# Windowed attention and a gated MLP on one core: accumulator banks as single tiles, and the first entry's loads in another order

## The chip, the cores and the metric

The kernel runs on one core of one Trainium2 chip. The metric is the device time of one execution in microseconds (us); lower is better. Engines: PE is TensorE (PEld its weight loads), DVE VectorE, ACT ScalarE, POOL GpSimd; SP is SyncE, whose queue here issues every transfer.

## The reference

```python
batch, n_heads, seq, head_dim = 8, 8, 576, 64
n_tokens, d_model, d_ff = 4608, 512, 2048
scores = q @ k.T / sqrt(64)
rel = pos[:, None] - pos[None, :]
plain   = (rel >= 0) & (rel < 32)                        # heads 0 to 3
dilated = (rel >= 0) & (rel < 128) & (rel % 4 == 0)      # heads 4 to 7
attn = softmax(where(mask, scores, -1e9))
x = (attn @ v), heads side by side: 4608 x 512
h = x @ w_in
out = (h * sigmoid(1.702 * h)) @ w_out
```

All inputs are float32.

## The kernel before

**Attention.** Heads are taken in pairs, one in each half of the partitions: 4 pairs for each of 8 batch entries. The host has reordered the dilated heads, so that both masks are bands. A score block is 32 queries by the 64 keys that its band can reach; `scores(k)` makes 18 such blocks per head and adds the mask by a matmul with the identity (`ident`). `softmax(k)` then takes the maxima (`mx`), subtracts them (`pr`), and takes exponentials, sums (`sm`) and quotients; two transposes (`ct`) and eight copies lay the result out as `bt`, which `product(k)` multiplies by values in windows of 96 keys for 64 queries (`av`, with a rest in the bank `sp`). `drain_x` writes x: for the first entry it is split at once into a high part `xh` and a low part `xl`.

**MLP.** Weights and activations are used as sums of a high and a low part in a faster matmul format, three matmuls for one product. Weights come as raw 64-bit words into buffers (`cell`, `second`), and `decode(n)` splits them with ACT and DVE: even n are blocks of w_in (`wih`, `wil`), odd n of w_out (`woh`, `wol`). The tokens make nine groups: eight of 512 (`m0` to `m7`, one per entry) and one of the eight rests of 64 (`r`). For each of 16 blocks f, `up(f)` makes 12 matmuls into the bank `hp`; `tanh`, `gate`, `hi_g` and `lo_g` make `gh` and `gl`; `down(f)` then adds 8 matmuls with `gh` and 4 with `gl` (the low parts) to the four results of the group, `acc`, which stand in four banks. PE does `up(f+1)` ahead of `down(f)`. At the last block each result is finished and drained (`ost`) in turn, and stored.

**Order.** All of it is written as operations with costs, keys that they read and write, and an urgency; `Plan.ordered` plays them through once at build time and emits each engine's instructions in the order that comes out. The waits between engines are then put in by the framework, by tile. In the first 30 us of the plan, idle stretches of PE are filled with matmuls on the identity (`warm`, written to the tile `idle`). Transfers all stand in SP's queue, in the plan's order. The first group's matmuls run while entry 1's attention and the rest of the weights are worked on.

**Places that the change touches.** The four results are halves of two tiles of two banks; in the first entry the scores of a pair use one of these tiles for both heads. Queries and keys of the first entry alternate between a buffer of their own (`qk`) and the unused space of `second` and `xm`; the values of pairs 1 to 3 lie in `second`, `xm` and `xr` until these are needed.

Of the kernel before, what the change touches and what calls it, by code (L numbers as in the profile page):

```python
# [17 lines left out]
P = 128  # L18
NC = DM // P
NF = DF // P  # L20
GT = 512
# [14 lines left out]
class Plan:  # L36
# [29 lines left out]
    def ordered(self, warm, warm_until):  # L66
# [21 lines left out]
        while any(open_):  # L88
            when, e = min((min(start(i, e) for i in open_[e]), e) for e in range(5) if open_[e])
            here = [i for i in open_[e] if start(i, e) <= when]  # L90
            i = min(here, key=lambda i: ops[i][1])
            e = min((k for k in ops[i][0] if start(i, k) <= when), key=lambda k: abs(ops[i][0][k]))
            for k in ops[i][0]:
                open_[k].remove(i)
            cost = abs(ops[i][0][e])
            if e == PE and when < warm_until:
                idle = max(0, int((when - max(free[e], 1.2)) / (0.24 if when > 5.0 else 0.44)))
                order.extend([(None, e)] * idle)
            order.append((i, e))
            if e == POOL or (e == DVE and ops[i][0][e] < 0):  # L100
                port[0] = when + cost

            free[e] = when + (cost if e != DMA else 0.7 if cost < 100 else 0.43)
            if e == DMA:
                bus[0] = max(bus[0], when + 2.0) + cost / 360.0
                cost = bus[0] - when
            for j in users[i]:
                for to in ready[j]:
                    gap = 0.0 if to == e == PE else 0.13 if to == e else LATENCY[to]
                    ready[j][to] = max(ready[j][to], when + cost + gap + ops[j][4])  # L110
                wait[j] -= 1
                if not wait[j]:
                    for to in ops[j][0]:
                        open_[to].add(j)
# [4 lines left out]
def tile_windowed_attention_then_gated_mlp(  # L119
# [92 lines left out]
    def decode(n, urgency):  # L212
# [42 lines left out]

    nq, nv = S, 2 * NW * D
    spare = [second.bitcast(F32).rearrange("p j n -> p (j n)"), xm.rearrange("p c n -> p (c n)"),
             xr[:, 1:].rearrange("p b c n -> p (b c n)")]
    late_v = words.bitcast(F32).rearrange("p j n -> p (j n)")
# [3 lines left out]
    def lots(k):  # L263

        if k < NC:
            return f"qk{k % 2}", f"v{k}"
        return ("qk0", "v0") if k < FIRST * NC or k % 2 == 0 else ("qk1", "v1")

    def load_qk(k):
        u, place = pairs[k], lots(k)[0]  # L270

        def work(e):
            if place == "qk0":
                flat = temp([P, 2 * nq], F32, "qk", f"qk_{k}")
                both = [flat[:, 0:nq], flat[:, nq:]]
            else:
                both = [spare[a][:, nv:nv + nq] for a in range(2)] if k < NC else [spare[0][:, nq * a:nq * a + nq] for a in range(2)]
            u["q"], u["k"] = both
            if k and place == "qk0":
                load(flat.rearrange("p (a s) -> p a s", a=2), qk[k])  # L280
                return
            for rows in (slice(0, D), slice(D, P)) if k == 0 else (slice(0, P),):
                for a in range(2):
                    load(both[a][rows], qk[k, rows, a])

        add({DMA: 590}, k, work, waits(k), (place,))

    def load_v(k):
        u, place = pairs[k], lots(k)[1]

        def work(e):
            if place == "v0":
                flat = temp([P, nv], F32, "v", f"v_{k}")
            else:
                flat = spare[k - 1][:, 0:nv] if k < NC else late_v[:, 0:nv]
            u["v"] = flat.rearrange("p (a m d) -> p a m d", a=2, m=NW)
            load(u["v"][0:KW], vp[k])

        add({DMA: 442}, k, work, waits(k), (place,))

# [16 lines left out]
    def scores(k):  # L317
        u = pairs[k]
        u["sp"] = sp = bank([P, 2, GT], f"acc{k % 2}" if k < NC else "sp", f"sp_{k}")
        u["boxes"] = sp[:, :, 0:QT * W].rearrange("p a (t w) -> p a t w", t=QT)  # L320
        for a in range(2):
            if masked(k):
                T.matmul(u["boxes"][:, a], ident, mask if dilated(k) else plain, start=True, stop=False,
                         skip_group_check=True)
        for t in range(QT):
            for a, j in [(a, j) for a in range(2) for j in range(min(4, S // 32 - 4 * t))]:
                g, rows = 4 * t + j, slice(D * a, D * a + D)
                dst, keys = u["boxes"][32 * j:32 * j + 32, a, t], u["k"][rows]
                for w in (0, 32) if g == 0 else (0,):
# [5 lines left out]
    def softmax(k, urgency):  # L335
# [6 lines left out]
        def sp():  # L342
            return u["boxes"] if masked(k) else pr

# [3 lines left out]
        if not masked(k):  # L348
            mine = mask if dilated(k) else plain
            for n, tiles, cost in ((P, slice(0, QT - 1), 0.62), (D, slice(QT - 1, QT), 0.22)):  # L350
                add({DVE: cost}, urgency, lambda e, n=n, tiles=tiles: pair(
                    e, pr[0:n, :, tiles], u["boxes"][0:n, :, tiles],
                    mine[0:n, None, tiles].broadcast_to([n, 2, tiles.stop - tiles.start, W]), ALU.add),
                    score_banks(k), (PR,))
        add({DVE: 0.80}, urgency, lambda e: V.tensor_reduce(out=mx, in_=sp(), axis=AX.X, op=ALU.max),
            (*held, PR), (MX,))
        add({DVE: 0.80}, urgency, lambda e: pair(e, pr, sp(), across(mx), ALU.subtract), (*held, MX), (PR,))
        add({ACT: 0.75}, urgency, lambda e: A.activation(pr, pr, AF.Exp, scale=0.125), (), (PR,))  # L358
# [30 lines left out]
    def product(k):  # L389
# [7 lines left out]
        for m in range(NW):  # L397
            for a in range(2):
                rows = slice(D * a, D * a + D)
                dst = u["av"][rows, D * m:D * m + D] if m < NW - 1 else u["rest"][rows]  # L400
                T.matmul(dst, u["v"][0:KW, a, m], bt[0:KW, a, m], start=True, stop=True, skip_group_check=True)  # L401

# [5 lines left out]
    def drain_x(k, urgency):  # L408

        u, (b, c) = pairs[k], divmod(k, NC)  # L410
        freed = ("v2", "qk1") if b == 1 else ()

# [28 lines left out]
        for n, (part, src, other) in enumerate(rests):  # L441
            add({ACT: 0.22}, urgency, lambda e, part=part, src=src: copy(
                e, part(view(xr[:, b, c])), src()), (banks[other],), (f"xr{b}{c}.{n}", *(("v3",) if b == 1 else ())))

# [35 lines left out]
    class Group:  # L480
# [180 lines left out]
```

## Time and profile before

| | before |
|---|---|
| median of 3 runs | 930.05 us (929.17 to 931.56) |
| profiled execution | 926.54 us, of which the span is 924.8 |
| PE busy | 893.0 us, 97% of the span |
| PE weight loads | 721.5 us |
| DVE busy | 520.9 us |
| ACT busy | 322.1 us |
| moved by DMA | 61.97 MB, 67 GB/s over the span |
| first matmul of the first up-projection | at 49.35 us |

The span runs from the first to the last instruction of the profiled execution. In rows of the timeline the first number is the start in us, the second the length, and what stands in brackets is the idle time ahead of it with what ended it; matmuls overlap, so that their starts, not their lengths, give the pace. In groups of instructions, the numbers behind the bar are the busy time in us and the mean of one in ns. In the waits, the three numbers are the total in us, the number of times, and the longest.

### The profile page before, as it was taken

How to read it: one execution, taken by the hardware profiler on the slowest of the kernel's cores; microseconds unless marked ns; L12 is line 12 of the kernel's file. 1: busy time of each engine (PE TensorE's matmuls, PEld its weight loads, DVE VectorE, ACT ScalarE, POOL GpSimd, SP SyncE). 2: the span in 40 equal slices, each digit the busy share in tenths (PEclk: the TensorE clock that was granted, in tenths of full speed). 3: DMA queues.
4: the chain of work that ended last, by engine and by line, in shares of the span. 5: the costliest groups of instructions: out<-in, count | busy, mean ns of one | idle time of the engine just before them, and what ended most of it. 6: DMA issues, size and time to landing. Idle time of an engine off the chain costs nothing.

```text
span 924.8 us, 16833 instructions
## 1 busy us (share of the span) xinstructions
PE 893.0 (97%) x7139; PEld 721.5 (78%) x7139; DVE 520.9 (56%) x990; ACT 322.1 (35%) x595; POOL 40.2 (4%) x41
## 2 busy tenths in 40 slices
PE   7789999999999999999999999999999999999997
PEld 3477777888878887888788878888788878878885
DVE  5789988667466536763667366735733433343332
ACT  3788986334343114421432143312411221121111
POOL 1012022000000000000000000000000000000000
PEclk9889999999999999999999999999999999999999
DMA  8467863213041102210231022200100010000002
GB/s 252 106 189 202 250 210 114 92 46 91 1 136 46 45 1 96 86 46 1 91 90 48 1 69 69 90 1 21 46 1 1 1 46 1 0 12 35 1 0 46
DMA packets 37275, 61.97 MB, mean 67 GB/s; under 512 B 19920, under 2 KB 19920, under 8 KB 37200
## 3 DMA queue, kind: packets, MB, share of 16 engines
q1 hardware_dynamic: 37200, 60.90, 21.5%
q8 instruction: 56, 0.92, 0.4%
q14 instruction: 19, 0.16, 0.1%
HBM read 49.81 MB, written 9.44 MB: 64 GB/s over the span
## 4 chain that ended last, share of the span: by engine, by line
PE 94%; ACT 2%; DMA 2%; DVE 1%; issue 1%; SPq 1%; ACTq 0%
PE hp_m L509 38%; PE acc_m L550 13%; PE acc_m L546 13%; PE acc_m L547 12%; PE hp_r L509 5%; PE av L401 4%; PE sp L332 3%; PE acc_r L550 2%; PE acc_r L546 2%; PE acc_r L547 2%; PE idle L619 1%; DMA qk<-qk_dram 1%; ACT ost_m L196 1%; DMA bt<-ct 0%; PE sp L401 0%
## 5 line engine op out<-in xcount | busy, mean ns | idle before, releaser
L520 DVE SCALAR_TENSOR_TENSOR g_m<-g_m,hp_m 128x512 f32<-128x512 f32 x128 | 87.9, 687 | 220.8 <-ACT g_m L517 220.4
L509 PE MATMUL hp_m<-xh,wih 128*128 128x512 f32 x512 | 201.9, 394 | 4.7 <-DVE xl L203 2.4
L546 PE MATMUL acc_m<-gh,woh 128*128 128x512 f32 x512 | 201.1, 393 | 0.5 <-ACT gh L196 0.5
L509 PE MATMUL hp_m<-xh,wil 128*128 128x512 f32 x512 | 200.3, 391 | 0.0
L509 PE MATMUL hp_m<-xl,wih 128*128 128x512 f32 x512 | 200.2, 391 | 0.0
L547 PE MATMUL acc_m<-gh,wol 128*128 128x512 f32 x512 | 199.4, 389 | 0.0
L517 ACT ACTIVATE g_m<-hp_m 128x512 f32<-128x512 f32 x128 | 76.5, 597 | 314.1 <-PE hp_m L509 313.9
L550 PE MATMUL acc_m<-gl,woh 128*128 128x512 f32 x512 | 143.9, 393 | 7.7 <-ACT ost_m L196 6.9
L550 PEld LDWEIGHTS acc_m<-gl,woh 128*128 128x128 f32 x512 | 95.7, 188 | 32.0 <-ACT ost_m L196 11.1
L509 PEld LDWEIGHTS hp_m<-xh,wih 128*128 128x128 f32 x512 | 96.7, 189 | 26.0 <-DVE g_m L520 3.2
L546 PEld LDWEIGHTS acc_m<-gh,woh 128*128 128x128 f32 x512 | 96.1, 188 | 21.8 <-ACT gh L196 1.4
L509 PEld LDWEIGHTS hp_m<-xl,wih 128*128 128x128 f32 x512 | 96.6, 189 | 20.4
L509 PEld LDWEIGHTS hp_m<-xh,wil 128*128 128x128 f32 x512 | 96.6, 189 | 19.9
L547 PEld LDWEIGHTS acc_m<-gh,wol 128*128 128x128 f32 x512 | 96.2, 188 | 19.5
L203 DVE TENSOR_TENSOR gl<-g_m,gh 128x512 fp32r<-128x512 f32 x124 | 87.7, 707 | 13.8 <-ACT gh L196 5.8
L196 ACT ACTIVATE bt<-ct 32x320 f32<-32x320 f32 x110 | 51.6, 469 | 30.1 <-DVE ct L368 28.3
L198 DVE CAST gh<-g_m 128x512 fp32r<-128x512 f32 x105 | 44.8, 427 | 8.8 <-PE acc_m L547 0.5
L520 DVE SCALAR_TENSOR_TENSOR g_r<-g_r,hp_r 128x512 f32<-128x512 f32 x16 | 11.0, 688 | 56.4 <-ACT g_r L517 56.4
L196 ACT ACTIVATE xm<-av 128x512 f32<-128x512 f32 (+2 forms) x42 | 22.8, 613 | 53.1 <-PE av L401 53.1
L358 ACT ACTIVATE pr<-pr 128x640 f32<-128x640 f32 x32 | 23.7, 739 | 49.7 <-DVE pr L203 49.6
L198 DVE COPY bt<-ct 32x320 f32<-32x320 f32 x106 | 33.7, 318 | 5.7 <-PE idle L401 3.4
L517 ACT ACTIVATE g_r<-hp_r 128x512 f32<-128x512 f32 x16 | 9.6, 598 | 73.4 <-PE hp_r L509 73.4
(117 smaller groups left out, 881.3 us busy)
## 6 DMA issues: line engine op xcount, KB each, us to landing
qk<-qk_dram SPq DMA_DIRECT2D x17, 576.0 KB, 5.3
out_dram<-ost_m SPq DMA_DIRECT2D x32, 256.0 KB, 2.0
second<-qk_dram SPq DMA_DIRECT2D x26, 288.0 KB, 4.2
v<-vp_dram SPq DMA_DIRECT2D x17, 432.0 KB, 4.1
cell<-wi_dram SPq DMA_DIRECT2D x11, 512.0 KB, 4.8
cell<-wo_dram SPq DMA_DIRECT2D x11, 512.0 KB, 4.3
words<-vp_dram SPq DMA_DIRECT2D x12, 432.0 KB, 3.8
second<-wi_dram SPq DMA_DIRECT2D x5, 512.0 KB, 4.0
```

The lines of the kernel that those rows point to most:

```text
L196: A.activation(dst, src, AF.Copy, scale=scale)
L198: V.tensor_copy(out=dst, in_=src)
L203: (V if e == DVE else G).tensor_tensor(out=dst, in0=a, in1=b, op=op)
L332: T.matmul(dst[:, w:w + n], u["q"][rows, 32 * g:32 * g + 32], keys[:, at:at + n], start=not masked(k), stop=True, tile_position=(D * a, 32 ...
L358: add({ACT: 0.75}, urgency, lambda e: A.activation(pr, pr, AF.Exp, scale=0.125), (), (PR,))
L401: T.matmul(dst, u["v"][0:KW, a, m], bt[0:KW, a, m], start=True, stop=True, skip_group_check=True)
L509: T.matmul(hps[f], st[:, f, c], mv[:, c], start=c == 0 and k == 0, stop=c == NC - 1 and k == 2)
L517: A.activation(self.g32, hps[f], AF.Tanh, scale=0.851)
L520: V.scalar_tensor_tensor(out=self.g32, in0=self.g32, scalar=1.0, in1=hps[f], op0=ALU.add, op1=ALU.mult)
L546: T.matmul(self.acc[j], woh[:, f, cols], gh, start=f == 0, stop=False)
L547: T.matmul(self.acc[j], wol[:, f, cols], gh, start=False, stop=False)
L550: T.matmul(self.acc[j], woh[:, f, P * j:P * j + P], self.g[f][1], start=False, stop=f == NF - 1)
```

## The change

Four edits, of which the last two go together:

- In `down`, each of the four results is a tile of one bank, and its first matmul waits for that bank alone.
- In the first entry, each head's scores have a bank and a tile of their own, and maximum and subtraction are done head by head.
- Queries and keys of a pair are loaded by one transfer (two for pair 0), into three buffers in turn (`qk`, `second`, `xm`); values are loaded head by head, two transfers for a pair. Pair 3's second head lies in `cell2`, the buffer of the first load of w_in's block 1 (n = 2), which therefore waits for pair 3's product. The urgencies of these loads are spread, so that the plan orders them otherwise.
- Fewer fillers are put into PE's gaps: 40 in place of 83 ahead of the first up-projection.

```diff
-                idle = max(0, int((when - max(free[e], 1.2)) / (0.24 if when > 5.0 else 0.44)))
+                idle = max(0, int((when - max(free[e], 1.2) - 1.5) / (0.28 if when > 5.0 else 0.44)))
...
-        taken = ("qk1", "v1") if n in (8, 9) else ()
+        taken = {2: ("v3",), 8: ("qk1", "v1"), 9: ("qk1", "v1")}.get(n, ())
...
-            return f"qk{k % 2}", f"v{k}"
+            return f"qk{k % 3}", f"v{k}"
...
+            u["q"], u["k"] = flat[:, 0:nq], flat[:, nq:2 * nq]
             for rows in (slice(0, D), slice(D, P)) if k == 0 else (slice(0, P),):
-                for a in range(2):
-                    load(both[a][rows], qk[k, rows, a])
-        add({DMA: 590}, k, work, waits(k), (place,))
+                load(flat[rows, 0:2 * nq].rearrange("p (a s) -> p a s", a=2), qk[k, rows])
+        add({DMA: 590}, 1.6 * k - 2.0, work, waits(k), (place,))
...
-            load(u["v"][0:KW], vp[k])
-        add({DMA: 442}, k, work, waits(k), (place,))
+            for a in range(2):
+                load(u["v"][a][0:KW], vp[k, :, a])
+        add({DMA: 442}, 1.6 * k - 0.3, work, waits(k), (place,))
...
-        u["sp"] = sp = bank([P, 2, GT], f"acc{k % 2}" if k < NC else "sp", f"sp_{k}")
+        if k < NC:
+            u["sp"] = [bank([P, GT], name, f"sp_{k}_{name}") for name in score_banks(k)]
+        else:
+            u["sp"] = bank([P, 2, GT], "sp", f"sp_{k}")
...
+        if k < NC:
+            for a in range(2):
+                add({DVE: 0.45}, urgency, lambda e, a=a: V.tensor_reduce(
+                    out=mx[:, a], in_=u["box"][a], axis=AX.X, op=ALU.max), (held[a], PR), (f"{MX}.{a}",))
+                add({DVE: 0.45}, urgency, lambda e, a=a: pair(
+                    e, pr[:, a], u["box"][a], mx[:, a, :, None].broadcast_to([P, QT, W]), ALU.subtract),
+                    (held[a], f"{MX}.{a}"), (PR,))
...
-                if f == 0 and j % 2 == 0:
-                    both = bank([P, 2, GT], f"acc{j // 2}", f"acc_{self.name}_{j}")
-                    self.acc[j], self.acc[j + 1] = both[:, 0], both[:, 1]
+                if f == 0:
+                    self.acc[j] = bank([P, GT], f"acc{j}", f"acc_{self.name}_{j}")
...
-                more = (f"acc{j + 1}",) if f == 0 and j % 2 == 0 else ()
-                add({PE: 0.454}, 0.0, lambda e: hi(j), (f"wo{f}", f"gh{f % 2}"), (f"acc{j}", *more))
+                add({PE: 0.454}, 0.0, lambda e: hi(j), (f"wo{f}", f"gh{f % 2}"), (f"acc{j}",))
```

What that does to the order, at three places. First PE at the end of group m1, at its last block, before; `acc_m_0` holds results 0 and 1, `acc_m_2` results 2 and 3, and what a row waits for stands in brackets:

```order
L550 MATMUL acc_m_0_1750<-gl_75,woh 128x512
L546 MATMUL acc_m_2_1818<-gh_73,woh 128x512
L547 MATMUL acc_m_2_1818<-gh_73,wol 128x512
L550 MATMUL acc_m_2_1818<-gl_75,woh 128x512
L546 MATMUL acc_m_2_1818<-gh_73,woh 128x512
L547 MATMUL acc_m_2_1818<-gh_73,wol 128x512
L550 MATMUL acc_m_2_1818<-gl_75,woh 128x512 [waits Activation_49]
L509 MATMUL hp_m_1_2727<-xh,wih 128x512 [waits DVE_49]
```

The same place after:

```order
L562 MATMUL acc_m_1_1731<-gl_75,woh 128x512
L558 MATMUL acc_m_2_1795<-gh_73,woh 128x512
L559 MATMUL acc_m_2_1795<-gh_73,wol 128x512
L562 MATMUL acc_m_2_1795<-gl_75,woh 128x512
L558 MATMUL acc_m_3_1801<-gh_73,woh 128x512
L559 MATMUL acc_m_3_1801<-gh_73,wol 128x512
L562 MATMUL acc_m_3_1801<-gl_75,woh 128x512
L522 MATMUL hp_m_1_2708<-xh,wih 128x512 [waits DVE_49]
```

The rows are the same matmuls in the same order; the wait for ACT at result 3's last matmul is gone.

SP's queue from its start, before (`wi` and `wo` are blocks of w_in and w_out, `vp` the values):

```order
L284 DMA qk_119<-qk_dram 64x576 x4
L297 DMA v_124<-vp_dram 96x1152
L284 DMA second<-qk_dram 128x576
L284 DMA xm<-qk_dram 128x576
L297 DMA second<-vp_dram 96x1152
L297 DMA xm<-vp_dram 96x1152
L297 DMA xr<-vp_dram 96x1152
L243 DMA cell_115<-wi_dram 128x512
L280 DMA qk_181<-qk_dram 128x1152
L284 DMA second<-qk_dram 128x576
L284 DMA xm<-qk_dram 128x576
```

and after, where `qk_180` is pair 3's:

```order
L279 DMA qk_119<-qk_dram 64x1152 x2
L279 DMA second<-qk_dram 128x1152
L297 DMA v_123<-vp_dram 96x576 x2
L279 DMA xm<-qk_dram 128x1152
L297 DMA second<-vp_dram 96x576
L297 DMA xr<-vp_dram 96x576
L297 DMA xm<-vp_dram 96x576
...
L244 DMA cell_115<-wi_dram 128x512
...
L297 DMA cell_117<-vp_dram 96x576
L279 DMA qk_180<-qk_dram 128x1152
```

Pair 1's and pair 2's queries and keys have moved to the front, pair 3's stay last, in `qk`. (Two more loads of values into `xr` are left out where the dots stand.)

PE behind the first up-projection, before: the score matmuls of pair 4 follow it, and then the second up-projection.

```order
L509 MATMUL hp_m_0_594<-xl,wih 128x512
L323 LDWEIGHTS ident
L323 MATMUL sp_621<-plain,ident 128x320
...
L332 MATMUL sp_621<-qk_582 32x64 x31
L509 MATMUL hp_m_1_667<-xh,wih 128x512
```

After, the first four results of the group stand between the two, the first two of them here, with the high part of the gate:

```order
L522 MATMUL hp_m_0_569<-xl,wih 128x512
L328 LDWEIGHTS ident
L328 MATMUL sp_593<-plain,ident 128x320
...
L337 MATMUL sp_593<-qk_557 32x64 x31
L558 MATMUL acc_m_0_643<-gh_72,woh 128x512
L559 MATMUL acc_m_0_643<-gh_72,wol 128x512
L558 MATMUL acc_m_1_646<-gh_72,woh 128x512
L559 MATMUL acc_m_1_646<-gh_72,wol 128x512
...
L522 MATMUL hp_m_1_658<-xh,wih 128x512
```

The second up-projection has moved behind the results of block 0.

More of the change, by code (lines that the diff above doesn't have):

```diff
@@ L272, in work @@
         def work(e):
-            if place == "qk0":
+            flat = {"qk0": None, "qk1": late, "qk2": main_x}[place]
+            if flat is None:
                 flat = temp([P, 2 * nq], F32, "qk", f"qk_{k}")
[L275 to L281, printed above, removed]
+            u["q"], u["k"] = flat[:, 0:nq], flat[:, nq:2 * nq]
             for rows in (slice(0, D), slice(D, P)) if k == 0 else (slice(0, P),):
-                for a in range(2):
-                    load(both[a][rows], qk[k, rows, a])
-        add({DMA: 590}, k, work, waits(k), (place,))
+                load(flat[rows, 0:2 * nq].rearrange("p (a s) -> p a s", a=2), qk[k, rows])
+        add({DMA: 590}, 1.6 * k - 2.0, work, waits(k), (place,))
     def load_v(k):
@@ L291, in work @@
         def work(e):
-            if place == "v0":
-                flat = temp([P, nv], F32, "v", f"v_{k}")
-            else:
-                flat = spare[k - 1][:, 0:nv] if k < NC else late_v[:, 0:nv]
-            u["v"] = flat.rearrange("p (a m d) -> p a m d", a=2, m=NW)
-            load(u["v"][0:KW], vp[k])
-        add({DMA: 442}, k, work, waits(k), (place,))
+            if k >= NC and place == "v1":
+                u["v"] = [late_v[:, nv * a:nv * a + nv] for a in range(2)]
+            elif 0 < k < NC:
+                u["v"] = [(None, late, main_x, left_x)[k][:, 2 * nq:2 * nq + nv],
+                          cell[:, 0:nv] if k == 3 else left_x[:, nv * (k - 1):nv * k]]
+            else:
+                flat = temp([P, 2 * nv], F32, "v", f"v_{k}")
+                u["v"] = [flat[:, nv * a:nv * a + nv] for a in range(2)]
+            u["v"] = [v.rearrange("p (m d) -> p m d", m=NW) for v in u["v"]]
+            for a in range(2):
+                load(u["v"][a][0:KW], vp[k, :, a])
+        add({DMA: 442}, 1.6 * k - 0.3, work, waits(k), (place,))
     def waits(k):
@@ L318, in scores @@
         u = pairs[k]
-        u["sp"] = sp = bank([P, 2, GT], f"acc{k % 2}" if k < NC else "sp", f"sp_{k}")
-        u["boxes"] = sp[:, :, 0:QT * W].rearrange("p a (t w) -> p a t w", t=QT)
+        if k < NC:
+            u["sp"] = [bank([P, GT], name, f"sp_{k}_{name}") for name in score_banks(k)]
+        else:
+            u["sp"] = bank([P, 2, GT], "sp", f"sp_{k}")
+            u["all"] = u["sp"][:, :, 0:QT * W].rearrange("p a (t w) -> p a t w", t=QT)
+        u["box"] = [(u["sp"][a] if k < NC else u["sp"][:, a])[:, 0:QT * W].rearrange("p (t w) -> p t w", t=QT)
+                    for a in range(2)]
         for a in range(2):
             if masked(k):
-                T.matmul(u["boxes"][:, a], ident, mask if dilated(k) else plain, start=True, stop=False,
+                T.matmul(u["box"][a], ident, mask if dilated(k) else plain, start=True, stop=False,
                          skip_group_check=True)
@@ L327, in scores @@
                 g, rows = 4 * t + j, slice(D * a, D * a + D)
-                dst, keys = u["boxes"][32 * j:32 * j + 32, a, t], u["k"][rows]
+                dst, keys = u["box"][a][32 * j:32 * j + 32, t], u["k"][rows]
                 for w in (0, 32) if g == 0 else (0,):
@@ L342, in sp @@
         def sp():
-            return u["boxes"] if masked(k) else pr
+            return u["all"] if masked(k) else pr
         def across(x):
@@ L400, in product @@
                 dst = u["av"][rows, D * m:D * m + D] if m < NW - 1 else u["rest"][rows]
[L401 removed]
+                T.matmul(dst, u["v"][a][0:KW, m], bt[0:KW, a, m], start=True, stop=True, skip_group_check=True)
     def spare_bank():
@@ L442, in drain_x @@
             add({ACT: 0.22}, urgency, lambda e, part=part, src=src: copy(
-                e, part(view(xr[:, b, c])), src()), (banks[other],), (f"xr{b}{c}.{n}", *(("v3",) if b == 1 else ())))
+                e, part(view(xr[:, b, c])), src()), (banks[other],), (f"xr{b}{c}.{n}", *(("v1", "v2", "v3") if b == 1 else ())))
     def parts(k):
```

17 lines of the change are left out of this document (9 added, 8 removed).

## The prediction

> **What bounds the kernel now.** I read the page's busy times first, then TensorE's waits, then its timeline at the two kinds of place where it stands still, and last the table by stages.
>
> ```profile
> span 924.8 us, 16833 instructions
> PE 893.0 (97%) x7139; PEld 721.5 (78%) x7139; DVE 520.9 (56%) x990; ACT 322.1 (35%) x595; POOL 40.2 (4%) x41
> ```
>
> TensorE (PE) is busy for 893.0 of 924.8 us, and the change takes no matmul of the real work away. All that can be won is among 32 us of idle time and in stretches at a lower clock. The waits of PE, longest in total first (total, times, longest):
>
> ```profile
> PE acc_m L550 <- ACT ost_m L196: 6.9, 10, 0.7
> PE av L401 <- ACT bt L196: 3.3, 1, 3.3
> PE sp L332 <- DMA qk<-qk_dram: 2.9, 2, 2.3
> PE hp_m L509 <- DVE xl L203: 2.4, 1, 2.4
> PE hp_m L509 <- DVE g_m L520: 2.2, 3, 1.0
> PE sp L332 <- issue: 1.6, 1, 1.6
> PE acc_m L550 <- DVE ost_m L200: 0.8, 1, 0.8
> PE acc_r L550 <- ACT ost_r L196: 0.7, 1, 0.7
> ```
>
> Three of these rows are one thing: the last low part of a result (line 550) waits until ScalarE or VectorE has drained another result. That happens 10+1+1 = 12 times, 8.4 us idle. The others belong to the opening (scores, products, first up-projection) and to the first group. One of the twelve, from PE's timeline, and the last one:
>
> ```profile
> 260.06 0.39 PE L546 MATMUL acc_m<-gh,woh 128*128 128x512 f32 x1
> 260.29 0.39 PE L547 MATMUL acc_m<-gh,wol 128*128 128x512 f32 x1
> 261.36 0.50 PE L550 MATMUL acc_m<-gl,woh 128*128 128x512 f32 x1 [0.69 <-ACT ost_m L196]
> 261.70 0.40 PE L509 MATMUL hp_m<-xh,wih 128*128 128x512 f32 x1
> ...
> 917.22 0.39 PE L547 MATMUL acc_r<-gh,wol 128*128 128x512 f32 x1
> 918.34 0.50 PE L550 MATMUL acc_r<-gl,woh 128*128 128x512 f32 x1 [0.74 <-ACT ost_r L196]
> ```
>
> Matmuls start 0.23 apart (260.06, 260.29). Around the wait they start 1.07 and 0.34 apart, so a wait costs 0.84+0.11 = 0.95 us, more than the 0.69 of idle time shown, since the pipeline empties. The last one has nothing behind it: 1.12-0.23 = 0.89.
>
> The opening, from the same timeline, with one row of VectorE (DVE) and one of the chain that ended last:
>
> ```profile
> 6.93 11.47 DMA qk<-qk_dram
> 18.44 1.10 PE L332 MATMUL sp<-qk 64*32 64x32 f32 x76 [2.31 <-DMA qk<-qk_dram]
> 20.96 1.37 PE L332 MATMUL sp<-xm,second 64*32 64x32 f32 x75
> 23.97 0.24 PE L332 MATMUL sp<-xm,second 64*32 64x64 f32 x1 [1.64 <-issue]
> 24.25 0.82 DVE L355 TENSOR_REDUCE mx<-sp 128x10 f32<-128x640 f32 x1 [2.99 <-PE sp L332]
> 24.46 1.15 PE L401 MATMUL av<-bt,v 96*64 96x64 f32 x32
> 49.35 0.77 PE L509 MATMUL hp_m<-xh,wih 128*128 128x512 f32 x1 [2.43 <-DVE xl L203]
> ```
>
> Pair 2's queries and keys land at 18.40, since 3,392 KB stand ahead of them in the one queue (576 + 4 x 432 + 576 + 512). Pair 3's scores should end at about 22.3, but their last matmul comes at 23.97: PE waited 1.64 us for nothing that the profile names. The product of pair 0 stands behind them in PE's order, and the first matmul of the up-projection comes 49.35-24.21 = 25.1 us after their end.
>
> The stages (length, busy time of PE, PEld, DVE, ACT, POOL, granted clock, DMA share, GB/s):
>
> ```profile
> 15.00:20.00 5.00, 2.69 (x84) 1.51 (x83) 3.09 (x10) 2.83 (x4) 0.00 (x0) 0.92 1.01 321
> 20.00:25.00 5.00, 3.36 (x99) 2.03 (x99) 2.01 (x5) 0.74 (x1) 1.41 (x2) 0.74 0.36 143
> 45.00:50.00 5.00, 2.57 (x34) 2.31 (x35) 3.89 (x9) 3.73 (x10) 0.00 (x0) 0.50 0.85 274
> 80.00:120.00 40.00, 38.98 (x376) 31.55 (x376) 37.65 (x73) 37.32 (x59) 6.16 (x5) 1.00 0.78 226
> 200.00:400.00 200.00, 198.63 (x1891) 163.23 (x1890) 122.57 (x240) 67.61 (x138) 5.21 (x5) 1.00 0.19 60
> ```
>
> While the first group runs, the weights are still being split: DVE is busy 94%, ACT 93% of 80 to 120, and PE 97%. All three are near their limit there. From 200 on only PE is.
>
> **Part A: result banks as four single tiles.** In the order before, result 3's last matmul waits on ScalarE, because results 2 and 3 are halves of one tile and the drain of 2 is an earlier reader of it; in the order after, the row has no wait. A wait that is gone gives 0.95: 11 x 0.95 + 0.89 = 11.3; one of the eleven is the row of 0.8 on DVE, with 0.1 more: **-11.4 us**. What is late next: the first matmuls of the next group's results wait for the drains of the same tiles, but 12 matmuls of an up-projection (12 x 0.23 = 2.7 us) stand between, and a drain takes 0.60. Bounds: 0 if each wait comes back behind it, -11.4 at most.
>
> **Part B: the first loads.** Both orders bring 4 x 576 KB of queries and keys, 4 x 432 KB of values and one 512 KB weight block before pair 3 can be scored, 4,544 KB, and pair 3's keys are the last of them in both. The queue is full all that time (DMA share 1.01), so the last 576 KB come 1.84 us (at the row's 321 GB/s) after 18.40, at 20.2. What changes is that pair 2's scores are long done by then, so PE starts pair 3's at once, not at 20.96. With 1.1 to 1.4 us for the scores they end at about 21.5, against 24.21: **-2.7 us**, if the 1.64 us of waiting doesn't recur there. DVE stood idle for 2.99 before that reduction, so 3.0 is the most; the least is 0, with the same wait at the same place. I take -2.7, for the wait seen follows from how fast PE gets through its instructions beside a full DMA queue, and pair 3's scores now come after 14 filler matmuls.
>
> The fewer fillers (40 in place of 83 before the first group) cost nothing by themselves, since PE is waiting there; their effect on the clock is a rival.
>
> **Part C: maxima and differences by head.** Per pair two reductions and two subtractions of 128x320 take the place of two instructions of 128x640, in the first entry alone. These rows, by shape, price them:
>
> ```profile
> L355 DVE TENSOR_REDUCE mx<-sp 128x10 f32<-128x640 f32 x5 | 4.1, 823 | 9.5 <-PE sp L332 9.5
> L203 DVE TENSOR_TENSOR pr<-sp,mx 128x640 f32<-128x640 f32 x5 | 4.1, 821 | 0.1
> L203 DVE TENSOR_TENSOR pr<-pr,sm 128x320 f32<-128x320 f32 x6 | 2.7, 485 | 0.0
> ```
>
> Half the elements take 485 where the whole takes 821. So 4 x 0.485 = 1.94 against 1.64, 0.3 more per pair, **+1.2 us** of DVE for four. Bounds: 0 (halves at half price, or in its gaps) to 1.2. I take 1.2 as on the path, for DVE has no room in the first group, where the work it puts off must be done.
>
> **Part D: what the first group gives back.** Weight block 1's load waits now for pair 3's product, since half of pair 3's values lies in its buffer: SP issues it behind all eight small copies of the first entry, not behind two. So its up-projection stands behind the first four results in PE's order, and these need the gate of block 0: ScalarE and DVE work that PE formerly covered with matmuls. The nearest row is PE's wait for the gate, up to 1.0. Beside that, an opening that ends 2.7 earlier doesn't end the splitting of weights earlier, and DVE and ACT have 2.4 and 2.7 us of room in those 40. I take all of B as given back, **+2.7**; bounds 0 and 2.7.
>
> Later entries load a pair's values in two transfers of 216 KB and odd pairs' queries and keys in one: cost 0, at a DMA share of 0.19 and with a pair in hand. Without that cover a transfer's time would show as a wait of PE's scores.
>
> **The sum** is -11.4-2.7+1.2+2.7 = -10.2 us. The profiled execution takes 926.54 (924.8 and 1.7 around it), and would take 916.3. It lies 3.5 under the median of the runs, 930.05; I leave that difference as it is: 930.05-10.2 = 919.8.
>
> **Rules of the Trainium skill.** The row of 1.64 us says that PE can lack instructions. The page "Runtime: NRT & Kernel Launch" of the Trainium skill (Instruction fetch mechanics) says that they come in blocks of 256, the next fetched while one is executed, "mostly hidden". By that rule the stall moves to pair 2's scores, as three pairs' scores now follow each other without fillers; the trace agrees so far that the time was not always hidden, and the sum stays, for DVE has pairs 0 and 1 to work on then.
>
> The clock row of 45 to 50 (0.50) stands beside PE's long waits of 3.3 and 2.4. The Trainium skill's "TensorE: Matmul & The Clock Gate" (Part 1: The HAM clock gate) says that a window of some 3.4 us with little work halves the clock; it speaks against taking fillers out, and the rows agree. It is the second rival below.
>
> **Rivals.**
> 1. The opening's gain is kept, since PE in the first group still has matmuls of other blocks to go on with, and DVE's 1.2 hides: 930.05-11.4-2.7 = 916.0. For it: DVE and ACT have 2.4 us of room in 40; against: it is near what B needs, in the best case.
> 2. Waits for the gate come close together in the first group, and PE drops to half its clock for a time. In 45 to 50 it ran at 0.50 all the time; one more such stretch of 5 us loses 2.5, and the wait of 1.0 that brings it comes on top: 919.8+3.5 = 923.3. For it: the waits of 1.0 on the gate. Against: with three of them the clock stayed at 1.00 from 60 on.
> 3. Part A isn't won: the wait moves to the next group's first results or to the gate behind four drains on ScalarE. Then 930.05+1.2 = 931.3, within 0.3%. Against: the 2.7 us of matmuls between.
> 4. Slower: weights are late throughout the first group, as block 1's load stands so late and SP's queue goes in order, so the later blocks' loads follow it. Each up-projection that waits costs 1.0 of idle time and 0.1 of restart; 16 of them 17.6: 930.05-11.4+1.2+17.6 = 937.5. It makes the kernel slower by over 0.3% (2.8 us, about what a measurement tells from no change) from 12 blocks on, (10.2+2.8)/1.1. For it: DVE and ACT at 94 and 93%. Against: the blocks' number and cost are unchanged, and before only three waited.
>
> **How the numbers follow.** Forecast 919.8: 0.50. Rival 1: 0.20, rival 2: 0.18, rival 3: 0.05, rival 4: 0.04; 0.03 for a gain of another size. Faster: 0.50+0.20+0.18+0.03 = 0.91; same 0.05; slower 0.04. The range takes in rivals 1 and 2 with 1 us beyond them for the spread of the runs (929.17 to 931.56): 915.0 to 924.5; outside are rivals 3 and 4 and some of the edges, under 0.2.
>
> **What would show it.** A: no row of the low part waiting for a drain, and an up-projection 0.23 after the last low part at a group's end. B: pair 3's scores end at 21 to 22, the first up-projection starts at 46 to 47. C: 128x320 reductions of about 0.49. D: PE's waits for the gate over 2.2 us in total in the first group. I am wrong if waits for drains appear on line 558 (the next results' first matmuls), if 1.6 us or more of unnamed waiting falls on pair 3 or the products, or if the first group is longer by over 6 us.

## The result, and the profile after

The changed kernel takes 918.9 us (median of four runs, 917.16 to 920.26), against 929.6 for the kernel before beside it: 0.9883 of its time, interval 0.9857 to 0.991. That is 10.7 us less; the forecast was 10.2. Its profiled execution took 920.26, of which the span is 918.5, 6.3 under the span shown of before.

The head of its page, and four of TensorE's waits (total, times, longest):

```profile
span 918.5 us, 16806 instructions
PE 882.0 (96%) x7096; PEld 718.5 (78%) x7096; DVE 520.6 (57%) x1004; ACT 322.1 (35%) x590; POOL 38.3 (4%) x40
```

```profile
PE av L414 <- DVE bt L199: 4.4, 1, 4.4
PE hp_m L522 <- DVE g_m L533: 3.6, 3, 1.5
PE sp_acc L337 <- issue: 2.4, 1, 2.4
PE acc_m L558 <- ACT gh L197: 1.2, 1, 1.2
```

No row of the low part (now line 562) waits for a drain any more; before there were twelve waits, 8.4 us. Waits for the gate (line 533) and for `gh` are new or longer, and the unnamed wait has moved to another pair and grown. The end of m1, from TensorE's timeline, where 0.84 was lost before:

```profile
262.85 0.39 PE L559 MATMUL acc_m<-gh,wol 128*128 128x512 f32 x1
263.07 0.39 PE L562 MATMUL acc_m<-gl,woh 128*128 128x512 f32 x1
263.30 0.39 PE L522 MATMUL hp_m<-xh,wih 128*128 128x512 f32 x1
```

Steps of 0.22 and 0.23: nothing waits. In the opening, however, the same view shows no gain:

```profile
14.87 1.15 PE L337 MATMUL sp_acc<-xm 64*32 64x32 f32 x63 [2.53 <-DMA xm<-qk_dram]
18.45 0.53 PE L337 MATMUL sp_acc<-xm 64*32 64x64 f32 x13 [2.43 <-issue]
18.90 5.01 PE L630 MATMUL idle<-ident 128*128 128x512 bf16 x14
24.38 1.00 PE L337 MATMUL sp_acc<-qk 64*32 64x32 f32 x76 [0.20 <-DMA qk<-qk_dram]
49.32 0.76 PE L522 MATMUL hp_m<-xh,wih 128*128 128x512 f32 x1 [3.07 <-DVE xl L204]
```

Pair 2's scores were cut by 2.43 us for which the view names no cause (the experiments below show that TensorE lacked instructions), fillers followed to 23.8, and pair 3's scores came at 24.38, as its keys landed. The first up-projection started at 49.32, before at 49.35.

Since one trace can mislead, most readings below are stages of the span, from the starts of three matmuls in the timeline: the first of the first up-projection, the first of group m1, and the last of the last result. A second number is a second trace of the same kernel.

| kernel | opening | first group | m1 to the last result | rest | span |
|---|---|---|---|---|---|
| before | 49.35, 51.42 | 102.64, 103.09 | 766.35, 766.64 | 6.46, 6.45 | 924.8, 927.6 |
| changed | 49.32, 47.63 | 107.26, 106.81 | 754.82, 754.83 | 7.10, 7.13 | 918.5, 916.4 |
| single tiles alone | 52.05 | 106.66 | 754.97 | 7.12 | 920.8 |
| loads alone | 46.92 | 105.14 | 765.66 | 6.48 | 924.2 |
| changed, old fillers | 48.67 | 107.13 | 754.94 | 7.16 | 917.9 |
| changed, block 1 early | 47.46, 47.71 | 103.17, 103.07 | 755.02, 754.49 | 7.05, 7.13 | 912.7, 912.4 |
| the same with double tiles | 44.23, 45.31 | 103.91, 104.39 | 766.50, 766.05 | 6.36, 6.45 | 921.0, 922.2 |

### The profile page after: what moved, and what is told of

Its sections match the earlier page's. It is cut to its first block, busy times and chain, and to the rows that moved or that the text cites. A ratio compares the mean times of both kernels' runs of the same rounds, so it can differ in the third digit from the quotient of the medians.

```text
span 918.5 us, 16806 instructions
## 1 busy us (share of the span) xinstructions
PE 882.0 (96%) x7096; PEld 718.5 (78%) x7096; DVE 520.6 (57%) x1004; ACT 322.1 (35%) x590; POOL 38.3 (4%) x40
## 4 chain that ended last, share of the span: by engine, by line
PE 89%; DMA 4%; DVE 2%; ACT 2%; issue 0%; SPq 0%; ACTq 0%
PE hp_m L522 36%; PE acc_m L558 12%; PE acc_m L562 12%; PE acc_m L559 12%; PE hp_r L522 5%; PE av L414 4%; PE sp L337 3%; PE acc_r L562 2%; PE acc_r L558 2%; PE acc_r L559 2%; DMA cell<-wo_dram 1%; DMA qk<-qk_dram 1%; DMA bt<-ct 1%; DMA cell<-wi_dram 1%; ACT cell L238 0%
## 5 line engine op out<-in xcount | busy, mean ns | idle before, releaser
L558 PEld LDWEIGHTS acc_m<-gh,woh 128*128 128x128 f32 x512 | 96.1, 188 | 22.3 <-ACT gh L197 1.6
L522 PEld LDWEIGHTS hp_m<-xh,wil 128*128 128x128 f32 x512 | 96.6, 189 | 20.9 <-DVE wil L204 1.0
L562 PEld LDWEIGHTS acc_m<-gl,woh 128*128 128x128 f32 x512 | 95.7, 188 | 20.2
L371 ACT ACTIVATE pr<-pr 128x640 f32<-128x640 f32 x32 | 23.7, 740 | 48.5 <-DVE pr L204 48.4
```

Of the source, the lines that this page charges most:

```text
L522: T.matmul(hps[f], st[:, f, c], mv[:, c], start=c == 0 and k == 0, stop=c == NC - 1 and k == 2)
L558: T.matmul(self.acc[j], woh[:, f, cols], gh, start=f == 0, stop=False)
L562: T.matmul(self.acc[j], woh[:, f, P * j:P * j + P], self.g[f][1], start=False, stop=f == NF - 1)
```

## The experiments

**Single tiles alone.** The kernel before, with the results' and scores' tiles and the halved maxima and differences of the change; loads, buffers and fillers as before.

```diff
-            both = bank([P, 2, GT], f"acc{j // 2}", ...)   # loads stay qk{k % 2}, v{k}
+            self.acc[j] = bank([P, GT], f"acc{j}", ...)
...
```

> The kernel before with the single tiles alone: four result tiles, and in the first entry a tile for each head's scores with maxima and differences by head. Loads, buffers and fillers are those of before. Theory 1 (twelve waits of 0.95 us go, and that is nearly the whole of the gain): 929.6-11.4+1.2 = 919.4, ratio 0.989, no row of the low part waiting for a drain, and the first up-projection at 49 us or 1 us later. Rival (only the idle time shown, 8.4 us, is won, and the loads bring the rest of the 10.7): 929.6-8.4+1.2 = 922.4, ratio 0.992.

Measured: 923.24 (919.96 to 923.81), 0.9944 of before (0.9926 to 0.9962), more than either theory gave, though the first one's waits are gone. The later groups gain all of part A (766.5 to 754.97), but opening and first group together are 5.5 longer than the mean of the two traces of before. Two of its waits:

```profile
PE hp_m L522 <- DVE g_m L533: 3.5, 2, 2.1
PE av L414 <- DVE bt L198: 4.6, 1, 4.6
```

So a first group that waits for the gate does not need the late block 1 that part D blamed: with the old loads, the plan's new order of VectorE's work is enough.

**Loads alone.** The changed kernel with double tiles, pairwise maxima and the fillers' rule of before.

```diff
-                    self.acc[j] = bank([P, GT], f"acc{j}", ...)
+                    both = bank([P, 2, GT], f"acc{j // 2}", ...)   # loads as changed, block 1 late
...
```

> The kernel before with the new loads, their buffers and the later load of weight block 1 alone; results and scores in double tiles and the fillers as before. Theory 1: the opening ends no earlier and the first group loses, so 929.6+0 to +4, ratio 1.000 to 1.004, with twelve waits for drains. Rival (the loads bring 2 to 3 us): 927, ratio 0.997.

Measured: 926.0 (923.87 to 932.36), 0.9987 (0.9968 to 1.0007): no difference that can be told. The opening is 3.5 shorter, the first group 2.3 longer, and eleven of the twelve waits for drains are there, ten in this row and one for `ost_r`:

```profile
PE acc_m L550 <- ACT ost_m L197: 6.9, 10, 0.7
PE hp_m L509 <- DVE g_m L520: 1.6, 1, 1.6
PE acc_m L546 <- ACT gh L197: 1.5, 3, 0.6
```

**The changed kernel with the old fillers.**

```diff
-   idle = max(0, int((when - max(free[e], 1.2) - 1.5) / (0.28 if when > 5.0 else 0.44)))
+   idle = max(0, int((when - max(free[e], 1.2)) / (0.24 if when > 5.0 else 0.44)))
```

> The changed kernel with the filler rule of before, so that PE has fillers between the first pairs' scores again. If PE's wait of 2.43 us in pair 2's scores comes from its going through three pairs' scores with nothing between, it gets shorter here or goes, the order of the transfers being the same; the time stays within 1.5 us of the changed kernel's 918.9, since pair 3's keys land no sooner. If the missing fillers cost clock in the opening, it is faster by 1 to 2 us. In either case, the rate of the transfers from 5 to 20 us (224 to 264 GB/s in the changed kernel's profile, 265 to 321 before) shows whether the new order of loads is slow by itself: again under 270 if so, 265 to 321 if that execution was an exception.

Measured: 920.27 (917.95 to 922.39), 0.9916 (0.9897 to 0.9935). Its interval overlaps that of the changed kernel, and its stages lie within 0.3 of it or between its two traces: the number of fillers is not where the time went. The transfers of 5 to 20 us ran at 260, 273 and 253 GB/s in stretches of 5 us, against 301, 265 and 321 before. From 15 to 20 us every trace with the new loads shows 223 to 264 GB/s and the three with the old ones 286 to 366: the new order of loads is slower in that stretch, and not in one execution alone.

**Block 1 early.** The changed kernel, with pair 3's second head in other free space, so that `cell2` is free and block 1's first load is issued behind two of the small copies, as before.

```diff
-  taken = {2: ("v3",), 8: ("qk1", "v1"), 9: ("qk1", "v1")}.get(n, ())
+  taken = {8: ("qk1", "v1", "v3"), 9: ("qk1", "v1", "v3")}.get(n, ())
...
-  cell[:, 0:nv] if k == 3 else ...
+  late[:, 2 * nq + nv:2 * nq + nv + 5 * D] if k == 3 else ...   # the other 4 windows in a tile of their own
```

> The changed kernel with the second head of pair 3's values in other free space (320 values in one buffer, 256 in a small new one, one transfer more), so that weight block 1 is loaded and split early and its up-projection stands again ahead of block 0's results. Theory 1 (the first group lost some 4 us to the late block 1): 918.9-3 = 916, ratio to before 0.985, and PE's waits in 50 to 130 fall from 6.7 us to under 4. Rival (the first group loses because ScalarE and VectorE have no room, wherever block 1 stands): 918.9, waits of PE unchanged in sum.

Measured: 912.76 (911.56 to 914.65), 0.9836 (0.9816 to 0.9856), the fastest kernel here, with a larger gain than theory 1 named. Its wait for the gate, and the stretch of 50 to 130 us (length, busy time of PE, PEld, DVE, ACT, POOL, clock, DMA share, GB/s) of three kernels:

```profile
PE hp_m L530 <- DVE g_m L541: 1.6, 3, 0.7
```

The kernel before:

```profile
50.00:130.00 80.00, 77.23 (x706) 61.45 (x705) 72.55 (x138) 70.88 (x110) 13.23 (x10) 0.98 0.69 203
```

The changed kernel:

```profile
50.00:130.00 80.00, 73.28 (x686) 57.55 (x685) 67.06 (x133) 63.08 (x95) 13.93 (x10) 0.98 0.68 203
```

Block 1 early:

```profile
50.00:130.00 80.00, 77.99 (x710) 61.37 (x710) 69.03 (x133) 69.52 (x108) 14.74 (x11) 0.99 0.71 216
```

With block 1 late, TensorE loses 4 us in these 80 and ACT gets through 95 instructions in place of 110; with block 1 early both are back (77.99, 108). VectorE is not fuller in the slow case (67 of 80 against 69), it waits too: the order is what was lost, not throughput.

**Few fillers between pairs 2 and 3.** Block 1 early, with 4 fillers in place of 14 there.

```diff
+  idle = min(idle, 4) if 14.0 < when < 20.0 else idle
```

> The kernel with block 1's load early (912.8), but with 4 filler matmuls in place of 14 between the scores of pairs 2 and 3. There the trace had pair 2's scores ending at 18.6 after a wait of 2.2 us for instructions, the 14 fillers at 0.43 each up to 23.1, and pair 3's scores from 23.30 with nothing to wait for, though their keys had landed at 21.4. Theory 1, the fillers hold pair 3 after the wait for instructions: scores of pair 3 start when the keys land, at 21.5 to 21.8, the first up-projection comes 1.6 earlier, at 45.9, and the time is 911.2. Theory 2, VectorE is the bound from pair 2 on, and pair 3's scores stand in a bank until it comes to them (its second reduction of pair 2 came only at 23.40): scores 1.6 earlier, the first up-projection at 47.5 as before, 912.8. Theory 3, the fillers are needed for the clock: the stretch at half clock that follows the wait for instructions lasts into the products, the first up-projection at 48 or later, over 913.3.

Measured: 915.3 (913.0 to 916.2), 0.9859 (0.9838 to 0.988).

```profile
17.58 0.53 PE L346 MATMUL sp_acc<-xm 64*32 64x64 f32 x13 [1.37 <-issue]
18.04 1.89 PE L639 MATMUL idle<-ident 128*128 128x512 bf16 x4
22.03 1.38 PE L346 MATMUL sp_acc<-qk 64*32 64x32 f32 x76 [1.57 <-DMA qk<-qk_dram]
23.34 2.17 PE L423 MATMUL av<-bt,v 96*64 96x64 f32 x32
```

Pair 3's scores start 1.3 earlier, but they and the product behind them run slower (1.38 for what took 1.00, 2.17 for a product of 1.15). The first up-projection comes at 48.07, not earlier. Theory 1 fell; the numbers are those of the third. The 21.4 that the forecast gives for the keys of the trace with 14 fillers is not in it: issued at 15.46, they took 7.2 us and landed at 22.7, so that the fillers held pair 3 back by 0.6 there, not by 1.9.

**The changed kernel a second time.** No edit.

> The changed kernel as it is, for a second trace. In the first one the opening won nothing (first up-projection at 49.31, before 49.35), since pair 3's keys landed at 24.3; the transfers of 5 to 20 us ran at 264, 223 and 239 GB/s in three stretches of 5 us, and those of the kernel before at 265 to 321. Theory 1, that slow stretch belonged to that execution: keys land by 22, first up-projection at 47.5 to 48.7 (the values of the two kernels with the same loads), and the first group stays 107, so span 917. Theory 2, it belongs to this order of loads: landing at 24 again, 49.3, span 918.5. In both theories the median stays 918 to 920.

Measured: 918.27 (917.65 to 920.58), 0.9902 (0.9882 to 0.9922).

```profile
16.57 0.52 PE L337 MATMUL sp_acc<-xm 64*32 64x64 f32 x13 [2.90 <-issue]
17.08 0.49 DVE L362 TENSOR_REDUCE mx<-sp_acc 128x5 f32<-128x320 f32 x1 [4.00 <-PE sp_acc L337]
22.74 1.00 PE L337 MATMUL sp_acc<-qk 64*32 64x32 f32 x76
47.63 0.76 PE L522 MATMUL hp_m<-xh,wih 128*128 128x512 f32 x1 [3.05 <-DVE xl L204]
```

Pair 3's scores wait for no data here, and the opening is 1.7 shorter: the late keys of the first trace belonged to that execution. The first group is as long as in it. VectorE's row is the one to read: it stood idle 4.00 us for pair 2's scores, most of it while TensorE lacked instructions.

**Double tiles with block 1 early, twice.** Block 1 early, but results and scores in double tiles with pairwise maxima and differences.

> The kernel with block 1's load early (912.8), but with result banks as halves of double tiles again, and scores, maxima and differences of the first entry by pairs, as in the kernel before. Theory 1, the parts add: 11.4 of waits come back, 0.6 of it is saved in the tail, and 4 pairs save 0.3 each on VectorE if that is on the path: 12 waits of line 558 for drains, 912.8+10.8-1.2 = 922.4. Rival: part of the single tiles' gain belongs to the order that they allow in the first group, and it grows by more without them: first group over 104 and 924 or more.

> The kernel with early block 1 and double tiles again, for a second trace. In the first one the first up-projection came at 44.23, 3.2 to 3.5 earlier than in the two traces with single tiles and halved maxima and differences (47.46, 47.71); but that execution was the fastest of its six. Theory 1, the halves cost VectorE time on the opening's path: 44 to 45 again, span 921 to 922. Theory 2, the first trace was a lucky one: 46.5 to 48, span 923.5 to 925.

Measured: 924.39 (922.83 to 925.8), 0.9962 (0.9945 to 0.9978), and 923.15 (920.39 to 923.96), 0.9945 (0.9928 to 0.9961). The waits for drains are all back, in both traces with the same row:

```profile
PE acc_m L558 <- ACT ost_m L197: 7.6, 11, 0.7
```

The opening is at 44.23 and 45.31, against 47.46 and 47.71 with single tiles: 2.8 in the mean, more than the two traces of either kernel differ (1.1 and 0.3). The first group is 1.0 longer in return. The second forecast's theory 1 is missed by 0.2 in span (922.2) and by 0.3 in the opening, theory 2 by 1.2 or more in each. Of the first, the medians lie 0.8 and 2.0 above the 922.4 of theory 1; what the rival named (first group over 104, 924 or more) came once each, 104.39 in the second trace and 924.39 in the first median, so it isn't out: the first group is longer without the single tiles, by 1.0.

**Fillers up to the first up-projection.** Block 1 early, with the fillers' limit at 44 us of the plan.

```diff
-WARM = 30.0
+WARM = 44.0
```

> The kernel with block 1's load early (912.8), with filler matmuls up to 44 us of the plan in place of 30: 16 more between the products of pairs 2 and 3 and 6 more ahead of the first up-projection. There TensorE waited 4.1 and 2.4 us, ran at half clock from 38.3 to 52.0, and the first ten matmuls of the first up-projection came 0.43 apart in place of 0.23. Theory 1, the waits bring the half clock and the fillers end it: ten matmuls x 0.20, the first group 2.0 shorter (103.2 to 101.2), the first up-projection no later than 47.5, and 910.8. Theory 2, the clock falls all the same, or the fillers (22 x 0.21 = 4.6 us at full clock, 9.4 at half) hold up the products behind them: first up-projection 1 to 3 us later, 913 to 916.

Measured: 913.62 (912.76 to 914.19), 0.9845 (0.9825 to 0.9865): no difference from the kernel without them, but not for want of an effect.

```profile
40.28 5.88 PE L638 MATMUL idle<-ident 128*128 128x512 bf16 x16 [2.60 <-DVE xl L204]
49.70 1.46 PE L638 MATMUL idle<-ident 128*128 128x512 bf16 x6 [2.35 <-DVE xl L204]
50.81 0.58 PE L530 MATMUL hp_m<-xh,wih 128*128 128x512 f32 x1
51.22 0.39 PE L530 MATMUL hp_m<-xh,wil 128*128 128x512 f32 x1
51.45 0.40 PE L530 MATMUL hp_m<-xl,wih 128*128 128x512 f32 x1
```

The half clock ended at 44.9 in place of 52.0, the first up-projection ran at 0.23, and the first group took 99.6, 3.5 less. But the fillers write to a bank that VectorE still reads, wait for it themselves (2.60, 2.35), and most of the 16 come at half pace ahead of the products: the opening is 3.2 longer. Both theories were half right.

**Narrow fillers.** Block 1 early, with 66 short matmuls ahead of the first scores and 40 between pairs 2 and 3; and, beside it, block 1 early again.

```diff
+NARROW = {2: 66, 16: 40}
...
+        if work is warm and fillers in NARROW:
+            for n in range(NARROW[fillers]):
+                T.matmul(..., ident[D * a:D * a + D, 0:32], ident[D * a:D * a + D, 0:32], ...)
```

> The kernel with block 1's load early (912.8), with 66 narrow filler matmuls (32x32) ahead of the first scores and 40 between those of pairs 2 and 3. In all traces with the new loads TensorE waits for instructions ahead of its 449th instruction, in pair 2's scores, and in those with the old loads ahead of its 705th, 256 later. The 66 (132 instructions) put the 449th ahead of pair 2's first score, where TensorE waits for keys anyway, and the 40 put the 705th ahead of pair 3's. Theory 1, the wait belongs to every 256th instruction and is on the path: no unnamed wait over 0.5 in the scores, pair 2's end at 16.2 to 16.6 (18.6), VectorE's first reduction of it at 16.3 (18.66), the first up-projection at 45 to 46 (47.46), and 911. Theory 2, the wait goes as said, but VectorE, ScalarE and the splitting of weights set the end of the opening: first up-projection at 47 to 48, 912 to 913.5. Theory 3, the wait does not belong to that instruction: it stays in pair 2's scores.

> The kernel with block 1's load early as it is, beside the one before it in this list, and for a second trace: 912 to 914, first up-projection at 46.5 to 48.5, first group 103 to 103.5. If its opening differs by more than 1.5 from the 47.46 of the first trace, differences of 1 to 2 us between openings of single traces say nothing.

Measured: 913.11 (910.87 to 916.54), 0.9838 (0.9811 to 0.9866), against 913.63 (912.39 to 915.13), 0.9844 (0.9823 to 0.9865): the same.

```profile
9.06 1.36 PE L346 MATMUL sp_acc<-second 64*32 64x32 f32 x75 [1.06 <-DMA second<-qk_dram]
13.24 0.26 PE L346 MATMUL sp_acc<-second 64*32 64x64 f32 x1 [2.82 <-issue]
14.08 1.38 PE L346 MATMUL sp_acc<-xm 64*32 64x32 f32 x76
21.82 1.00 PE L346 MATMUL sp_acc<-qk 64*32 64x32 f32 x76 [1.12 <-DMA qk<-qk_dram]
```

The wait moved with the count: 449 instructions of TensorE (weight loads and waits counted) stand ahead of it here and in both traces without the narrow ones, though it is now pair 1's last score. The trace also lists the packets of the queue that brings instructions: one of 16 KB runs from 10.45 to 11.72 here, inside the stop, and one from 13.79 to 15.00 in the second trace of the changed kernel, where TensorE stands still from 13.7 to 16.57. For which engine they are it does not say. Pair 2's scores end at 15.5 in place of 17.1 and 18.7; pair 3's, which now wait for their keys, at 22.8 in place of 24.2 and 24.3. The first up-projection comes at 46.53, 0.9 and 1.2 earlier, between the theories 1 and 2; the median does not move.

**The kernel before a second time.** No edit.

> The kernel before as it is, for a second trace: its first one (926.5) lies 3.5 under the first median and at the fast end of its runs. Theory 1, its executions differ in the opening, where transfers compete: the first up-projection at 51 to 53 in place of 49.35, first group 102.6 to 103, each later group 97.48 again, span 927 to 928. Theory 2, the first group differs: first up-projection at 49 to 50, first group 105 or more. If the first values come again (49.3, 102.6, 924.8), what the medians show beyond the traces stays open.

Measured: 927.86 (926.85 to 929.34), 0.9998 (0.9987 to 1.001); span 927.6.

```profile
51.42 0.76 PE L509 MATMUL hp_m<-xh,wih 128*128 128x512 f32 x1 [2.44 <-DVE xl L203]
```

The first theory holds: the trace that the prediction was made from had a short opening, by 2.1; the first group differs by 0.4.

## Why the prediction was right, and where it was not

The time was right, and the largest term with it. Along the path below two terms were off by about 2 us each, in opposite directions; that with the rest the gain came within 0.5 of the forecast is luck. In the means of the table's traces, the change's parts come apart as a chain of kernels: before (926.2), new loads with block 1 early and double tiles (921.6), single tiles (912.55), block 1 late (917.45, the changed kernel).

| step | opening | first group | m1 to last result | rest | sum | forecast |
|---|---|---|---|---|---|---|
| B, loads | -5.6 | +1.3 | -0.2 | -0.1 | -4.6 | -2.7 |
| A, results | | | -11.5 | +0.7 | -10.8 | -11.4 |
| C, heads | +2.8 | -1.0 | | | +1.8 | +1.2 |
| D, late block 1 | +0.9 | +3.9 | +0.1 | | +4.9 | +2.7 |

The sum is -8.7 or -8.8 (917.45-926.2), against medians that differ by 10.7 and 10.2 in the two comparisons; the 1.5 to 2 left over is within what executions of one kernel differ by, and no trace assigns it. Single and double tiles stand for A and C together; A is read from the later groups, where C does nothing, and C from the opening and first group. The 0.9 of D in the opening is less than the 1.7 by which the two traces of the changed kernel differ there. The prices hold for this order of steps only: on the old loads, A and C without B cost 5.5 ahead of m1, not 1.8. All six spans (two traces in the mean, or one, marked *; these and "before" have the old fillers):

| | old loads | new loads, block 1 late | new loads, block 1 early |
|---|---|---|---|
| double tiles | 926.2 | 924.2* | 921.6 |
| single tiles | 920.8* | 917.45 | 912.55 |

Single tiles win 5.4, 6.7 or 9.1, and the late block costs 2.6 on double tiles, which is what was forecast, and 4.9 on single ones. What nearly stays on every path is A in the later groups, 10.7 (with eleven waits to win) to 11.5.

**A.** The 0.95 for each wait is right within 0.03: from one group's first matmul to the next was 97.47 before (97.51 in the second trace) and is 96.53 now (m3 to m4, 450.23-352.76 = 97.47 and 450.89-354.36 = 96.53). What was missed is 0.7 behind the last result. Before, the waits had spread the last drains; now the last matmul ends earlier by its 0.89, but the final drains queue on ACT. The last drain of before, and the last two of now, which ACT does in one stretch:

```profile
918.88 0.60 ACT L196 ACTIVATE ost_r<-acc_r 128x512 f32<-128x512 f32 x1 [0.59 <-PE acc_r L550]
911.20 1.23 ACT L197 ACTIVATE ost_r<-acc_r 128x512 f32<-128x512 f32 x2 [0.31 <-PE acc_r L562]
```

Rival 3, that the waits return on the next results' first matmuls, is out: line 558 has only waits for `gh`.

**B.** The sign held, but not for the reason given. The forecast took 25.1 us from the end of pair 3's scores to the first up-projection as fixed, and had the scores end 2.7 earlier. From the rows of the timelines, end of pair 3's scores (start and length added) and distance to the first up-projection:

| kernel | pair 3's scores end | distance |
|---|---|---|
| before | 24.2, 24.9 | 25.1, 26.5 |
| changed | 25.4, 23.7 | 23.9, 23.9 |
| block 1 early | 24.3, 24.2 | 23.2, 23.5 |
| the same, narrow fillers | 22.8 | 23.7 |
| the same, double tiles | 23.7, 24.4 | 20.6, 20.9 |

The step that failed is the 21.5: the scores end no earlier than before, in the mean of two. Two things hold them, the missing instructions in pair 2 with 14 fillers behind them, and in one execution the keys. These were forecast for 20.2, at the rate of before, and landed at 24.3 (issued at 14.91) and 21.1 (issued at 12.56). All that the opening won, 1.9, was won in the distance, which stays within 0.3 or 0.4 for a kernel with the new loads and differs between the kernels of the table by up to 3.3: another order of VectorE's work. There the last product waits 3.5 to 5.3 us for copies of `bt` and the first up-projection 2.4 to 3.1 for `xl` in every trace with the new loads but the one with long fillers. Which step of the new loads shortens that chain no run here isolates. My bound of 3.0 looked at the scores alone, and the loads with block 1 early give 4.6.

**The missing instructions.** I let the rule of the Trainium skill, "Runtime: NRT & Kernel Launch" (Instruction fetch mechanics), move the stall to pair 2's scores at no cost. It did move there, and the blocks of 256 that the page states agree with the traces: 449 instructions ahead of it, or 705 in the kernel before, 256 apart. "Mostly hidden" does not agree: 1.4 to 3.0 us. My reason for a cost of nothing, that VectorE has pairs 0 and 1 to work on then, was wrong, since it stood idle 5.0 and 4.0 us there in the two traces of the changed kernel. With the wait out of pair 2's scores, the opening of the kernel with narrow fillers was 0.9 and 1.2 shorter; in its median that cannot be seen.

**C.** The instructions cost what the row of before said: VectorE's reductions and subtractions of the halves in the changed kernel (shortest, median, longest in ns),

```profile
L362 DVE TENSOR_REDUCE mx<-sp_acc x8: 430/488/494, 7.7 to 30.0; 128x5 f32<-128x320 f32 x8
L204 DVE TENSOR_TENSOR pr<-sp_acc,mx x8: 480/484/492, 8.2 to 30.5; 128x320 f32<-128x320 f32 x8
```

and the 1.8 on the path are near the 1.2, in a kernel whose opening hangs on VectorE. The extra instructions can't be all of it: ahead of m1 single tiles cost 3.7 where block 1 is late ("changed, old fillers" against "loads alone") and 5.5 on the old loads. How the order that they bring costs the rest is not shown.

**D.** The mechanism is right, the size was not, and it lay outside the bounds that I gave. The waits for the gate and `gh` are 4.8 in the rows shown and 4.9 in the second trace, over the 2.2 that I named. All gaps of TensorE in the first group behind its first up-projection are seven, 6.7 us together, in the first trace, against five of 2.8 in the first of before; (6.7-2.8) and two more restarts of 0.11 make 4.1 of the 4.6 by which it grew there (107.26-102.64). I had tied the price to what the opening gained, as if it were that gain given back. It is a price of its own: taking away the late load, with one small transfer more and all else kept, returns 4.9 in the traces and 4.6 to 6.1 in the medians. On double tiles the 2.7 would have been right (2.6). The waits for the gate or `gh` were four in the first trace and six in the second, the longest 1.5, half as long again as the 1.0 taken from the row of before. Rival 4, weights late throughout the group with 16 waits of 1.1, is out: in both traces the first group waits for weights twice, 1.1 in all.

**Rivals 1 and 2.** Rival 1 (the opening's gain kept) is out: the first group gave back more than it. Rival 2, a new stretch at half clock in the first group, did not come: from 60 to 900 us the granted clock is 1.00. The stretch around the first up-projection lasted 13.7 us in both traces of the changed kernel and 10.2 in those of before, but it covers most or all of that up-projection in all of them. There the Trainium skill's "TensorE: Matmul & The Clock Gate" (Part 1: The HAM clock gate) agrees with the long fillers: busy windows of its 3.4 us ended the stretch after 6.8 in place of 13.7.

The half pace did grow in the opening. Pair 1's 76 score matmuls, before and changed:

```profile
9.80 0.98 PE L332 MATMUL sp<-xm,second 64*32 64x32 f32 x76 [1.20 <-DMA xm<-qk_dram]
9.58 1.38 PE L337 MATMUL sp_acc<-second 64*32 64x32 f32 x76 [1.10 <-DMA second<-qk_dram]
```

With two fillers ahead of them in place of 13, they take 1.38 in place of 0.98, and the fillers behind pair 2 come 0.43 apart up to 22.3 us and 0.22 from 22.7 on. The clock column of the stages shows 1.00 there all the same; the trace has no record of the clock before 22.6, so the pace is what tells. With the old fillers pair 1's scores took 1.00 and the time was the same, so no cost of it is seen in the result.

## What to carry to other kernels

A false wait between halves of one tile has a price that can be read to a few hundredths from the starts around it, and it comes off almost in full where one engine is the bound; give each result that is drained alone a tile of its own. A buffer borrowed for a short-lived operand can cost more than the borrowing wins: ask which later load it holds back, and price the order that follows, not the load. And what follows a stage at a fixed distance in one order of the work need not keep that distance in another: which engine's chain the distance consists of is to be read before a gain is carried through it.

## What was not expected of the hardware

- TensorE's wait for instructions stands behind a fixed count (449 or 705 instructions) in every trace, whatever is there, and takes 1.4 to 3.0 us while the loads of the opening run. With 132 more instructions ahead it came 132 instructions earlier in the rest of the program.
- The same transfers with the same order of loads ran at 223 to 283 GB/s from 10 to 15 us in different executions and kernels, and pair 3's keys landed at 21.1 in one trace of the changed kernel and at 24.3 in the other. The opening of one kernel differs by 0.3 to 2.1 us between two traces, the later groups by at most 0.5 in 755 to 767.
- Fillers at half clock came 0.43 apart, twice as far as the 0.22 at full clock: 16 of them, eleven at half clock, took 5.88 us, and a gap that they were to fill was overrun.
